# Streaming attention and an expert layer on one core: block order, load pieces and row sums changed

## The chip, the cores and the metric

The kernel runs on one core of a Trainium2 chip. The metric is the device time of one execution in microseconds, read as the median of the runs. The engines named below are TensorE (PE: matmuls and transposes), VectorE (DVE), ScalarE (ACT), GpSimd (POOL) and SyncE (SP, which here only issues transfers).

## What is computed

Four batches, eight heads, 768 positions, head size 64. Each query sees the 128 last positions and the first four ("sinks"). The result, 3072 tokens of 512, goes through four experts whose outputs are added with weights per token.

```python
keep = (pos[None, :] < 4) | ((rel >= 0) & (rel < 128))
scores = np.where(keep, scale * q @ k.T, -1e9)
a = exp(scores - max); a = a / (sum(a) + 1e-9)
x = (a @ v) as (tokens, 512)
p = domain_probs / (domain_probs.sum(-1) + 1e-9)
out = sum over e of p[:, e] * (relu(x @ w1[e]) @ w2[e])     # w1: 512x1024, w2: 1024x512
```

## The kernel before

**Tiling.** A *unit* `u` is one block of 128 queries of one batch with all eight heads; there are 24, six per batch. Before the change they run in the order of the output: unit 0 to 5 are batch 0, and so on. A block sees its own 128 keys and those of the block before it. Blocks 0 and 1 of a batch hold the sinks among these keys; block 0 has one key block instead of two. Blocks 2 to 5 need the four sink keys in addition.

**One unit.** `load` (L213) fetches q, k and v of the block, `[128, 8, 64]` float32, by three transfers of 256 KB on SyncE's queue, each row in pieces of 256 bytes. `cast` (L200) makes bf16 of them on GpSimd. For the first eight units (`UPE`, `UPA`, `UPX`) TensorE transposes queries and keys (`pe_tr`, L286; units 0 and 1 in float32 and without the cast), and `q_out`, `k_out` copy the result from PSUM; later units use transposing transfers (`dma_q`, `dma_k`). `scores` (L340) multiplies, `maxima` (L352, VectorE) masks and takes the minimum of the negated scores, `exps` (L360, ScalarE) forms the exponentials and, through `accum_out`, the row sums; this makes a second instruction, a reader, for each exp. `pe_a`/`a_out` (L400) or `dma_a` (L387) transpose the weights, `values` (L420) multiplies with V, `sums` and `normalise` divide, and `pe_x`/`x_out` (L471) or `dma_x` (L463) write the transposed result `xT`, 512 tokens (four units) to a tile.

**Sinks.** For units below `UPS` = 8 with block 2 or higher, the sinks' weights are transposed with the others and a 128x512 matmul (L417) with a spread matrix `vsd` adds their values; `vsd` is built from eight small loads (L240) and a GpSimd product (L160). From unit 8 on, `weigh_sinks` (L186, L190) does this on GpSimd from a broadcast copy `vsb` of the four values (1 MB per batch, L170), seven operations of 128x512.

**Experts.** Items are `(tokens, expert)`: first four items of 128 tokens with expert 0, then 512 tokens at a time. `mm1` (L495, tile `hpsum`), `relu` (L509, L507), `mm2` (L521, tile `mopsum`) and `collect` (L558 to L562) make one item. w1 and w2 of an expert are loaded by GpSimd's queue with a conversion to bf16 (L228, L231), each tied to a cast (`w_after`).

**What sets the order.** Every step is a node with a cost on an engine, its dependencies and a due time (`want`). A list scheduler written in the kernel takes the node that can start first by its own clock and emits the instructions in that order; `MOVED` holds hand-made shifts of due times, and loads, first and second matmuls keep fixed sequences. Where TensorE would idle at the start, `keep_busy` (L482) emits filler matmuls. Each engine runs its own list in order.

Of the kernel before, what the change touches and what calls it, by code (L numbers as in the profile page):

```python
# [16 lines left out]
def kernel(  # L17
# [43 lines left out]
    UPS = 8  # L61

    UG = 4

    UF = 2
# [12 lines left out]

    NBS = -(-(UPS - 2) // NQB)
    vs = resid.tile([HS, B, D], FP32, name="vs", tag="vs")  # L80
    vsd = [resid.tile([P, H, D], BF16, name=f"vsd{b}", tag=f"vsd{b}") for b in range(NBS)]
# [3 lines left out]
    dp_nat = consts.tile([NTB, P, E], FP32, name="dp_nat")  # L85


    Abuf = [resid.tile([P, 2 * H + 1, P], BF16, name=f"A{i}", tag=f"A{i}") for i in range(2)]
# [3 lines left out]
    qTb = [resid.tile([P, NHP, P], BF16, name=f"qT{i}", tag=f"qT{i}") for i in range(2)]  # L92
    skd = [resid.tile([P, NHP, 2, NSINK], BF16, name=f"skd{i}", tag=f"skd{i}") for i in range(2)]
# [48 lines left out]
    bd = consts.tile([HS, H], FP32, name="bd")  # L142

    def sink_consts(eng):
        for t in Abuf:
            nc.gpsimd.memset(t[:, 2 * H], 0.0)
        for t in vsd:
            nc.gpsimd.memset(t, 0.0)

# [3 lines left out]

    def sink_heads(eng):
        nc.vector.reduce_sum(
            out=bd, in_=ident[0:HS, 0:HS].rearrange("p (h r) -> p h r", r=NSINK), axis=AX.X
        )

    def sink_values(eng, b):
        nc.gpsimd.tensor_mul(  # L160
            vsd[b][0:HS], vs[:, b, :][:, None, :].to_broadcast([HS, H, D]),
            bd[:, :, None].to_broadcast([HS, H, D]),
        )
# [4 lines left out]
    def spread_values(eng, b):  # L168
        vsb[b] = at_sb.tile([P, H, NSINK, D], FP32, name="vsb", tag="vsb", bufs=1)
        nc.sync.dma_start(  # L170
            out=vsb[b].rearrange("p h r d -> p h (r d)"),
            in_=v[b, :, 0:NSINK, :].rearrange("h r d -> h (r d)")[None].to_broadcast(
                [P, H, NSINK * D]
            ),
        )

    def sinks_on_pool(u):
        return u >= UPS and u % NQB >= 2

    def weigh_sinks(eng, u):  # L180

        pr = Abuf[u % 2][:, 2 * H, 0:HS].rearrange("p (h r) -> p h r", r=NSINK)
        sv = at_sb.tile([P, H, D], FP32, name="sv", tag="sv", bufs=2)
        for r in range(NSINK):
            t = sv if r == 0 else at_sb.tile([P, H, D], FP32, name="svr", tag="svr", bufs=1)
            nc.gpsimd.tensor_mul(  # L186
                t, vsb[u // NQB][:, :, r], pr[:, :, r : r + 1].to_broadcast([P, H, D])
            )
            if r:
                nc.gpsimd.tensor_add(sv, sv, t)  # L190
        live["sv", u] = sv
# [26 lines left out]
    def cast(eng, u, what):  # L218
        t = raw.pop((what, u))
        if what == "v":  # L220
            vn[u] = resid.tile([P, H, D], BF16, name="vn", tag="vn", bufs=5)
            copy_on(eng, vn[u], t)
# [14 lines left out]

    def load_sinks(eng):
        for h in range(H):
            nc.sync.dma_start(  # L240
                out=vs[h * NSINK : (h + 1) * NSINK],
                in_=v[:, h, 0:NSINK, :].rearrange("b r d -> r b d"),
            )
# [23 lines left out]
    def queries_of(u):  # L267
        return qTb[u % 2]
# [6 lines left out]
    def dma_k(eng, u):  # L275
        b, qb = divmod(u, NQB)
# [5 lines left out]
    def pe_tr(eng, u, what):  # L282
        src = raw.pop((what, u)) if u < UF else nat.pop((what, u))
        ps = ps_s.tile([P, NHP, P], FP32 if u < UF else BF16, name="tr" + what, tag="s")
        for hp in range(NHP):
            nc.tensor.transpose(  # L286
                ps[:, hp], src[:, 2 * hp : 2 * hp + 2, :], identf if u < UF else ident
            )
        live["tr" + what, u] = ps

    def q_out(eng, u):
        copy_on(eng, qTb[u % 2], live.pop(("trq", u)))

    def k_out(eng, u):
        b, qb = divmod(u, NQB)
        copy_on(eng, keys_of(b)[:, :, qb], live.pop(("trk", u)))

    def sink_keys(eng, b):
        for c in range(2):
            r = slice(c * D, (c + 1) * D)  # L300
            copy_on(eng, skd[b % 2][r, :, c], kT[b][r, :, 0, 0:NSINK])

    def sink_scores(eng, u):
        ps = ps_s.tile([P, H, NSINK], FP32, name="ss", tag="s")
        for hp in range(NHP):
            nc.tensor.matmul(  # L306
                ps[:, 2 * hp : 2 * hp + 2], lhsT=qTb[u % 2][:, hp], rhs=skd[u // NQB % 2][:, hp],
# [23 lines left out]
    def scores(eng, u, g):  # L331

        b, qb = divmod(u, NQB)
        lo = 0 if qb else 1
        sp = {}
        for h in groups_of(u)[g]:
            if h % 2 not in sp:
# [3 lines left out]
                sp[h % 2][:, h // 2 % 2, lo:2], lhsT=qTb[u % 2][r, h // 2],  # L341
                rhs=kT[b][r, h // 2, qb - 1 + lo : qb + 1], start=True, stop=True,
# [3 lines left out]
    def maxima(eng, u, h):  # L346
        qb = u % NQB
        if ("negm", u) not in live:
            live["ssum", u] = at_sb.tile([P, H], FP32, name="ssum", tag="ssum", bufs=3)
# [8 lines left out]
    def exps(eng, u, h):  # L358
        lo = 1 if u % NQB == 0 else 0
        nc.scalar.activation(  # L360
            out=Abuf[u % 2][:, 2 * h + lo : 2 * h + 2, :], in_=SM[:, h, lo:2], func=AF.Exp,
            scale=-1.0, bias=live["negm", u][:, h : h + 1],
            accum_out=live["ssum", u][:, h : h + 1],
# [9 lines left out]
    def sink_exps(eng, u):  # L373
        nc.scalar.activation(  # L374
            out=Abuf[u % 2][:, 2 * H, 0:HS],
# [3 lines left out]
    def at_of(u):  # L379
        if ("AT", u) not in live:  # L380
            live["AT", u] = at_sb.tile([P, 2 * H + 1, P], BF16, name="AT", tag="AT", bufs=2)
        return live["AT", u]

    def dma_a(eng, u, half):
        lo = half * H
        hi = H if half == 0 else 2 * H + (1 if u % NQB >= 2 and not sinks_on_pool(u) else 0)
# [4 lines left out]
    def slots_of(u, hp):  # L391
        if hp == NHP:
            return [2 * H]
        return [4 * hp + i for i in range(4) if u % NQB > 0 or i % 2]
# [15 lines left out]
    def values(eng, u):  # L410
        b, qb = divmod(u, NQB)
        lo = 1 if qb == 0 else 0
        op = ps_s.tile([P, H, D], FP32, name="op", tag="s")
        at = live.pop(("AT", u))
        sinks = qb >= 2 and not sinks_on_pool(u)
        if sinks:
            nc.tensor.matmul(op, lhsT=at[:, 2 * H], rhs=vsd[b], start=True, stop=False)  # L417
        for h in range(H):
            for i in range(lo, 2):
                nc.tensor.matmul(  # L420
                    op[:, h], lhsT=at[:, 2 * h + i], rhs=vn[u - 1 + i][:, h, :],
                    start=(not sinks and i == lo),
                    stop=(i == 1 and (h == H - 1 or not sinks)),
                )
        live["op", u] = op

    def sums(eng, u):
        ssum = live.pop(("ssum", u))
        rs = at_sb.tile([P, H], FP32, name="rs", tag="rs", bufs=3)
        if u % NQB >= 2:  # L430
            rk = at_sb.tile([P, H], FP32, name="rk", tag="rk", bufs=3)
            nc.vector.reduce_sum(
                out=rk, in_=Abuf[u % 2][:, 2 * H, 0:HS].rearrange("p (h r) -> p h r", r=NSINK),
                axis=AX.X,
            )
            nc.vector.scalar_tensor_tensor(
                out=rs, in0=ssum, scalar=1e-9, in1=rk, op0=ALU.add, op1=ALU.add
            )
        else:
            nc.vector.tensor_scalar_add(rs, ssum, 1e-9)  # L440
# [3 lines left out]
    def normalise(eng, u):  # L444
        xn = at_sb.tile([P, H, D], BF16, name="xn", tag="xn", bufs=2)
        res = live.pop(("op", u))
        if sinks_on_pool(u):
            both = at_sb.tile([P, H, D], FP32, name="both", tag="both", bufs=1)
            nc.vector.tensor_add(both, res, live.pop(("sv", u)))  # L449
            res = both  # L450
        nc.vector.tensor_mul(  # L451
            xn, res, live.pop(("rs", u))[:, :, None].to_broadcast([P, H, D])
# [74 lines left out]
    def last_group(eng, i, sub):  # L527
# [4 lines left out]
        sc = live["shares"][:, tok // P, e : e + 1]  # L532
        at = 0
        for w, pool, tag in ((256, ps_o, "o"), (128, ps_h, "h"), (128, ps_o, "o")):
# [10 lines left out]
            nc.sync.dma_start(out=out[tok : tok + P, at : at + w], in_=dst[:, at : at + w])  # L545
            at += w

    def collect(eng, i, sub):
# [7 lines left out]
        sc = live["shares"][:, tok // P, e : e + 1]  # L556
# [9 lines left out]
    def store(eng, i, sub):  # L566
        tok = items[i][0] + sub * P
        nc.sync.dma_start(
            out=out[tok : tok + P, :], in_=out_sb[tok // 512][:, (tok % 512) // P, :]
# [32 lines left out]
    starts = [14.0, 20.0, 26.0, 32.0, 40.0, 56.0, 71.0]  # L602
# [12 lines left out]
    DMA_TILE = 0.19  # L615
    for u in range(NU):
        b, qb = divmod(u, NQB)
# [3 lines left out]
        for j, what in enumerate("qkv"):  # L621
            last = u - NRAW[what]
            free = ("cast", last, what)
            if last < UF and what != "v":
                free = ("tr" + what, last)
            deps = [(free, HOP)] if last >= 0 else []

            if u - AHEAD >= UPA:
                deps.append((("begun", "da", u - AHEAD, 1), HOP))
            node(("load", u, what), {"SP": 0.5}, lambda eng, u=u, w=what: load(eng, u, w), deps,  # L630
                 S0 - 24.0 + 0.1 * j, dma=1.0 if u < 2 else 1.1)
            deps = [(("load", u, what), HOP)]
            if u < UF and what != "v":
                continue
            if what == "v":
                if u >= 5:
                    deps.append((("av", u - 4), HOP))
            elif u >= UF + 2:
                prev = "tr" + what if u - 2 < UPE else "d" + what
                deps.append(((prev, u - 2), HOP))  # L640
            node(("cast", u, what), {"POOL": 0.56},
                 lambda eng, u=u, w=what: cast(eng, u, w), deps, S0 - 8.0 + 0.1 * j)
        qfree = [(("s", u - 2, len(groups_of(u - 2)) - 1), HOP)] if u >= 2 else []
        if u >= 2 and (u - 2) % NQB >= 2:
            qfree.append((("ss", u - 2), HOP))
        kfree = [(("s", (b - 1) * NQB - 1, 1), HOP)] if b >= 2 else []
# [390 lines left out]
```

## Time and profile before

| | |
|---|---|
| runs | 395.32, 502.31, 394.74 us; median 395.32 |
| profiled execution, span | 395.2 us, granted clock 1.000 |
| PE busy | 384.8 us (97%), 2513 instructions |
| DVE, ACT, POOL busy | 203.6 (52%), 225.6 (57%), 147.7 us (37%) |
| transfers | 51.95 MB in 148154 packets, 135548 of them under 512 bytes |

The page cuts the span into 40 slices and gives each engine's busy share in tenths. The chain of waits follows the work that ended last back to the start. A list in order of time has start, duration, engine, line, output and input, and in brackets the idle time ahead of an instruction and who ended it. A matmul's duration is longer than the distance to the next one, since they are pipelined.

### The profile page before, as it was taken

The numbers are of one execution on the slowest core, as the hardware profiler recorded it, in microseconds if no ns is written. First come the engines' busy times: TensorE is split into PE (matmuls) and PEld (weight loads), VectorE is DVE, ScalarE is ACT, GpSimd is POOL, SyncE is SP. The second block draws the span as 40 slices with busy tenths as digits, with TensorE's granted clock in tenths as the row PEclk, the third lists the DMA queues.
The fourth block names the chain that finished last, engine by engine and source line by source line (L and its number), as shares of the span: only waits on it lengthen the run. The fifth ranks groups of instructions, "written<-read, shape, count | busy, mean of one in ns | idle before, by whom it ended". The sixth has DMA issues, their size and how long they took to land.

```text
span 395.2 us, 7309 instructions
## 1 busy us (share of the span) xinstructions
PE 384.8 (97%) x2513; PEld 194.8 (49%) x2555; DVE 203.6 (52%) x672; ACT 225.6 (57%) x632; POOL 147.7 (37%) x177
## 2 busy tenths in 40 slices
PE   8999999999999999999999999999999999999996
PEld 6777555544444444444444444444444444444443
DVE  3996787259364853843866734456455332200233
ACT  5896787666573663764754746466377333354320
POOL 3515050309928561074495740154943800000000
PEclk9999999999999999999999999999999999999999
DMA  8998999918599689986555996762751300200002
GB/s 188 204 203 166 190 200 194 243 40 165 129 148 219 131 194 255 209 195 93 114 111 123 200 226 138 159 140 62 199 120 21 48 13 2 80 28 1 0 2 107
DMA packets 148154, 51.95 MB, mean 131 GB/s; under 512 B 135548, under 2 KB 143100, under 8 KB 148116
## 3 DMA queue, kind: packets, MB, share of 16 engines
q1 hardware_dynamic: 141844, 43.09, 51.2%
q0 software_dynamic: 6272, 8.39, 13.1%
q8 instruction: 20, 0.33, 0.3%
q14 instruction: 18, 0.15, 0.1%
HBM read 38.88 MB, written 6.29 MB: 114 GB/s over the span
## 4 chain that ended last, share of the span: by engine, by line
PE 86%; DMA 11%; issue 1%; POOL 1%; SPq 0%; DVE 0%; POOLq 0%
PE mopsum L521 40%; PE hpsum L495 39%; DMA rawk<-in_k_dram 5%; DMA rawv<-in_v_dram 5%; PE sp L340 3%; PE op L420 2%; DMA rawq<-in_q_dram 1%; PE lpsum L537 0%; PE tra L400 0%; PE trk L286 0%; PE trq L286 0%; PE ss L306 0%; POOL vn L200 0%; PE trx L471 0%; PE idle_out L482 0%
## 5 line engine op out<-in xcount | busy, mean ns | idle before, releaser
L495 PE MATMUL hpsum<-xT,w 128*128 128x512 bf16 (+1 forms) x843 | 182.5, 355 | 1.1
L521 PE MATMUL mopsum<-w,ht 128*128 128x512 bf16 x739 | 175.7, 379 | 1.6 <-issue 0.6
L509 ACT ACTIVATE ht<-hpsum 128x512 bf16<-128x512 f32 x172 | 102.0, 594 | 113.6 <-PE hpsum L495 100.8
L521 PEld LDWEIGHTS <-ht 128*128 128x128 bf16 x760 | 72.9, 98 | 87.7 <-issue 2.7
L495 PEld LDWEIGHTS <-w 128*128 128x128 bf16 x864 | 76.4, 98 | 79.0 <-issue 2.0
L562 DVE SCALAR_TENSOR_TENSOR out_sb<-mopsum,shares,out_sb 128x512 f32<-128x512 f32 x71 | 52.9, 746 | 109.2 <-PE mopsum L521 107.0
L360 ACT ACTIVATE A<-SM,negm 128x256 bf16<-128x256 f32 (+1 forms) x192 | 92.0, 481 | 16.6 <-DVE negm L352 13.6
L352 DVE CUSTOM_DVE_ANT_0 SM<-sp,M,slow 128x256 f32<-128x256 f32 x128 | 54.7, 479 | 8.6 <-PE sp L340 8.4
L190 POOL TENSOR_TENSOR sv<-sv,svr 128x512 f32<-128x512 f32 x36 | 45.6, 1267 | 2.8
L186 POOL TENSOR_TENSOR svr<-vsb,A 128x512 f32<-128x512 f32 x36 | 38.1, 1059 | 1.9
L200 POOL CAST qn<-rawq 128x512 bf16<-128x512 f32 x22 | 13.9, 634 | 62.1 <-DMA rawq<-in_q_dram 60.7
L360 ACT ACTIVATION_READ_ACCUMULATOR A<-SM,negm 128x1 f32 x192 | 36.3, 189 | 0.0
L186 POOL TENSOR_TENSOR sv<-vsb,A 128x512 f32<-128x512 f32 x12 | 13.0, 1082 | 62.5 <-ACT A L374 62.5
L558 ACT ACTIVATE out_sb<-mopsum,shares 128x512 f32<-128x512 f32 x19 | 13.0, 687 | 19.1 <-PE mopsum L521 19.0
L352 DVE CUSTOM_DVE_ANT_0 SM<-sp,M 128x128 f32<-128x128 f32 (+1 forms) x64 | 19.1, 351 | 5.9 <-PE sp L340 5.9
L200 POOL CAST kn<-rawk 128x512 bf16<-128x512 f32 x22 | 13.5, 614 | 19.7 <-DMA rawk<-in_k_dram 19.6
L200 POOL CAST vn<-rawv 128x512 bf16<-128x512 f32 x24 | 15.2, 633 | 12.5 <-DMA rawv<-in_v_dram 12.5
L449 DVE TENSOR_TENSOR both<-op,sv 128x512 f32<-128x512 f32 x12 | 8.3, 688 | 17.4 <-PE op L420 9.6
L340 PE MATMUL sp<-kT,qT 64*128 64x256 bf16 (+1 forms) x192 | 16.8, 271 | 0.0
L352 DVE DVE_READ_ACCUMULATOR2_ANT negm<- 128x1 f32 x192 | 15.9, 83 | 0.0
L420 PEld LDWEIGHTS <-AT 128*128 128x128 bf16 x352 | 13.4, 98 | 4.8 <-issue 0.2
L451 DVE TENSOR_TENSOR xn<-op,rs 128x512 bf16<-128x512 f32 x12 | 8.3, 688 | 14.5 <-PE op L420 14.1
(76 smaller groups left out, 197.5 us busy)
## 6 DMA issues: line engine op xcount, KB each, us to landing
w<-in_moe_w_dram POOLq DMA_DIRECT2D x8, 1024.0 KB, 12.8
rawq<-in_q_dram SPq DMA_DIRECT2D x24, 256.0 KB
rawk<-in_k_dram SPq DMA_DIRECT2D x24, 256.0 KB
rawv<-in_v_dram SPq DMA_DIRECT2D x24, 256.0 KB
out_dram<-out_sb SPq DMA_DIRECT2D x23, 256.0 KB
vsb<-in_v_dram SPq DMA_DIRECT2D x3, 1024.0 KB
AT<-A SPq DMA_TRANSPOSE x32
qT<-qn SPq DMA_TRANSPOSE x16
```

Of the source, the lines that this page charges most:

```text
L186: nc.gpsimd.tensor_mul(t, vsb[u // NQB][:, :, r], pr[:, :, r : r + 1].to_broadcast([P, H, D]))
L190: nc.gpsimd.tensor_add(sv, sv, t)
L200: nc.gpsimd.tensor_copy(out=out, in_=in_)
L340: nc.tensor.matmul(sp[h % 2][:, h // 2 % 2, lo:2], lhsT=qTb[u % 2][r, h // 2], rhs=kT[b][r, h // 2, qb - 1 + lo : qb + 1], start=True, sto ...
L352: nc.vector.tensor_tensor_reduce(out=SM[:, h][part], in0=live.pop(("sp", u, h))[part], in1=masks[min(qb, 2)], scale=-scale, scalar=live["s ...
L360: nc.scalar.activation(out=Abuf[u % 2][:, 2 * h + lo : 2 * h + 2, :], in_=SM[:, h, lo:2], func=AF.Exp, scale=-1.0, bias=live["negm", u][:, ...
L420: nc.tensor.matmul(op[:, h], lhsT=at[:, 2 * h + i], rhs=vn[u - 1 + i][:, h, :], start=(not sinks and i == lo), stop=(i == 1 and (h == H - ...
L495: nc.tensor.matmul(ps[:, j * n : (j + 1) * n], lhsT=w1[e][:, db, fb * P : (fb + 1) * P], rhs=xT[t0 // 512][:, db, t0 % 512 : t0 % 512 + n] ...
L509: nc.scalar.activation(out=ht, in_=ps, func=AF.Relu)
L521: nc.tensor.matmul(ps, lhsT=hidden(i, fb, sub), rhs=w2[e][:, fb, :], start=(fb == 0), stop=(fb == NFB - 1),)
L558: nc.scalar.activation(out=dst, in_=ps, func=AF.Copy, scale=sc)
L562: nc.vector.scalar_tensor_tensor(out=dst, in0=ps, scalar=sc, in1=dst, op0=ALU.mult, op1=ALU.add)
```

## The change

Six things change together.

- *Order.* Units 0 to 7 are now blocks 0 and 1 of batches 0 to 3; units 8 to 23 are blocks 2 to 5, batch by batch (`place`, `tile_of`). No unit below 8 needs sinks any more, and all 16 from unit 8 on take the GpSimd way: `vsd`, its loads and its matmul are gone, `vsb` is loaded four times instead of three. Keys and values of the first blocks are kept until their batch's turn (`kside`, `vk`, `move_keys`).
- *Loads.* q and k of two blocks come in one transfer of 512 KB, in pieces of 512 bytes; a partition then holds two neighbouring rows, and `every_other` puts the transposed columns back in order.
- *First units.* Units 0 and 1 are cast to bf16 like the others, on any of three engines, ahead of the transposes.
- *Row sums below unit 8.* V gets a 65th column of ones; `values` runs by halves of four heads, and `normalise_half` reads the sum from the product. The exps of these units have no `accum_out`.
- *Weights.* w1 and w2 are tied to other casts (`w_at`); q of unit 4 waits for w2 of expert 0, q of unit 6 for w1 of expert 1 (`BEHIND`).
- *Due times.* `starts`, `MOVED` and some costs of nodes have new numbers.

```diff
+    BEHIND = {4: ("w2", 0), 6: ("w1", 1)}
...
+    def place(u):
+        if u < UPS:
+            return divmod(u, 2)
+        b, qb = divmod(u - UPS, NQB - 2)
+        return b, qb + 2
...
     def sinks_on_pool(u):
-        return u >= UPS and u % NQB >= 2
+        return u >= UPS
...
     def load(eng, u, what):
-        b, qb = divmod(u, NQB)
-        t = resid.tile([P, H, D], FP32, name="raw" + what, tag="raw" + what, bufs=NRAW[what])
+        b, qb = place(u)
+        if u < UPS and what != "v":
+            t = resid.tile([P, 2 * H * D], FP32, name="raw" + what, tag="raw" + what, bufs=NRAW[what])
+            for j in range(2):
+                raw[what, u + j] = t.rearrange("p (h j d) -> p h j d", h=H, j=2)[:, :, j]
+            nc.sync.dma_start(
+                out=t.rearrange("p (h x) -> p h x", h=H),
+                in_=src_of[what][b, :, 0 : 2 * P, :].rearrange("h (p j) d -> p h (j d)", j=2),
+            )
+            return
...
+            full = resid.tile([P, H, D + 1], BF16, name=tag, tag=tag, bufs=bufs)
+            if u < UPS:
+                nc.gpsimd.memset(full[:, :, D : D + 1], 1.0)
+            copy_on(eng, full[:, :, 0:D], t)
...
+    def every_other(t, u):
+        return t.rearrange("p a s (c j) -> p j a (s c)", j=2)[:, u % 2]
...
     def q_out(eng, u):
-        copy_on(eng, qTb[u % 2], live.pop(("trq", u)))
+        copy_on(eng, every_other(qTb[u // 2 % 2], u), live.pop(("trq", u)))
...
+        total = {"accum_out": live["ssum", u][:, h : h + 1]} if u >= UPS else {}
...
+    def values(eng, u, heads=range(8)):
+        blocks = [(1, u)] if before(u) is None else [(0, before(u)), (1, u)]
+        w = D + 1 if u < UPS else D
+        op = ps_s.tile([P, len(heads), w], FP32, name="op", tag="s")
...
+    def normalise_half(eng, u, f):
+        op = live.pop(("op", u, 4 * f))
+        rs = at_sb.tile([P, 4], FP32, name="rsh", tag="rsh", bufs=3)
+        nc.vector.tensor_scalar_add(rs, op[:, :, D], 1e-9)
+        nc.vector.reciprocal(out=rs, in_=rs)
+        nc.vector.tensor_mul(
+            live["xn", u][:, 4 * f : 4 * f + 4], op[:, :, 0:D],
+            rs[:, :, None].to_broadcast([P, 4, D]),
+        )
...
-    w_after = [(2, "v"), (3, "v"), (4, "v"), (5, "v"), (6, "v"), (7, "v"), (10, "v"), (11, "v")]
+    w_at = [(2, 'q'), (3, 'q'), (3, 'v'), (4, 'v'), (6, 'q'), (6, 'k'), (8, 'k'), (12, 'q')]
```

More of the change, by code (lines that the diff above doesn't have):

```diff
@@ L385, in dma_a @@
         lo = half * H
-        hi = H if half == 0 else 2 * H + (1 if u % NQB >= 2 and not sinks_on_pool(u) else 0)
+        hi = lo + H
         nc.sync.dma_start_transpose(
@@ L615, with avs, norms, last_s @@
     DMA_TILE = 0.19
+    LOAD1 = 1.15
+    LOAD2 = 1.85
+    def avs(u):
+        return [("av", u, 0), ("av", u, 1)] if u < UPS else [("av", u)]
+    def norms(u):
+        return [("norm", u, 0), ("norm", u, 1)] if u < UPS else [("norm", u)]
+    def last_s(u):
+        return ("s", u, len(groups_of(u)) - 1)
+    def all_exps(u):
+        return [("exp", u, h) for h in range(H)]
+    def on(*lists):
+        return [(key, HOP) for keys in lists for key in keys]
+    rawat = {"q": [], "k": [], "v": []}
+    vnat = []
     for u in range(NU):
-        b, qb = divmod(u, NQB)
+        b, qb = place(u)
         pe = u < UPE
@@ L621 @@
         for j, what in enumerate("qkv"):
[L622 to L631, printed above, removed]
@@ L639 @@
+            deps = [(("load", u // 2 * 2 if pair else u, what), HOP)]
+            if what == "v":
+                if u >= UPS or u % 2 == 0:
+                    if len(vnat) >= NVN:
+                        deps += on(avs(vnat[-NVN]))
+                    vnat.append(u + 1 if u % 2 == 0 and u < UPS else u if qb == NQB - 1 else u + 1)
+            elif u >= 2:
                 prev = "tr" + what if u - 2 < UPE else "d" + what
                 deps.append(((prev, u - 2), HOP))
-            node(("cast", u, what), {"POOL": 0.56},
+            node(("cast", u, what),
+                 {"POOL": 0.56, "DVE": 0.38, "ACT": 0.58} if u < 2 and what != "v" else {"POOL": 0.66 if u < UPS and what == "v" else 0.56},
@@ L647 @@
+        kfree = on([last_s(UPS + 4 * (b - 2) + 3)]) if b >= 2 and u >= UPS else []
         if pe:
             for what in "qk":
[L649 to L654 removed]
@@ L658 @@
+            node(("ko", u), any_of(0.5, 0.36), lambda eng, u=u: k_out(eng, u),
+                 on([("trk", u)]), S0 - 2.0)
+            have = on([(x, 2 * (u // 2) + j) for x in ("qo", "ko") for j in range(2)])
         else:
@@ L821 @@
     node(("shares",), {"DVE": 0.8}, shares_out, [(("trs",), HOP)], 9.0)
-    MOVED = {
[4 rows of a table removed]
-    }
+    MOVED = {'ao': 6.8,
+     'da': -3.8,
+     'dq': 2.8,
+     'dx': -2.0,
+     'exp': 3.8,
+     'i0': -4.1,
+     'i1': 1.8,
+     'i10': -6.1,
+     'i11': -6.7,
+     'i2': 15.0,
+     'i3': 6.1,
+     'i4': 5.5,
+     'i5': 8.8,
+     'i6': -1.9,
+     'i7': 5.0,
+     'i9': -6.8,
+     'mm1': 0.5,
+     'mm2': 1.7,
+     'norm': -5.3,
+     'out': -7.2,
+     'relu': 15.1,
+     's': -8.2,
+     'ska': -30.8,
+     'sm': -3.5,
+     'ss': 1.0,
+     'sv': -0.9,
+     'trk': -7.2,
+     'trq': -2.9,
+     'u0': -9.9,
+     'u1': 1.6,
+     'u11': -2.2,
+     'u12': -18.9,
+     'u13': 9.5,
+     'u15': 10.9,
+     'u4': -31.5,
+     'u5': 12.8,
+     'u6': 16.9,
+     'u7': 4.5,
+     'u9': -3.6,
+     'x': 3.1,
+     'xT': -6.7}
     for key, d in nodes.items():
@@ L832 @@
             d["want"] += MOVED.get(f"i{key[1]}", 0.0) + MOVED.get(key[0], 0.0)
-        elif len(key) > 1 and key[0] not in ("w1", "w2", "load", "sk", "vsd", "vsb"):
+        elif len(key) > 1 and key[0] not in ("w1", "w2", "load", "sk", "kc", "vsb"):
             if key[1] < 9:
```

324 lines of the change are left out of this document (148 added, 176 removed), and 4 rows, old and new, of the table MOVED.

## The prediction

> **What bounds the kernel now.** I read the busy table by slices first, then TensorE's list in order of time, then the DMA and queue rows of the first 40 us. The profiled execution took 395.2 us, the median of the runs shown is 395.32; the sum is made against 395.2.
>
> ```profile
> PE   8999999999999999999999999999999999999996
> PEclk9999999999999999999999999999999999999999
> DMA  8998999918599689986555996762751300200002
> PE mopsum L521 40%; PE hpsum L495 39%; DMA rawk<-in_k_dram 5%; DMA rawv<-in_v_dram 5%; PE sp L340 3%; PE op L420 2%; DMA rawq<-in_q_dram 1%; PE lpsum L537 0%; PE tra L400 0%; PE trk L286 0%; PE trq L286 0%; PE ss L306 0%; POOL vn L200 0%; PE trx L471 0%; PE idle_out L482 0%
> ```
>
> The reader is to see that TensorE is full at the full granted clock (first and second row), and that all transfers on the chain of waits belong to q, k and v. They lie at its start. So the questions are how early useful matmuls start, how many there are, and where TensorE waits. Three places in TensorE's list, and the table by stretches:
>
> ```profile
> 26.46 0.72 PE L495 MATMUL hpsum<-xT,w 128*128 128x128 bf16 x10
> 67.59 0.59 PE L495 MATMUL hpsum<-xT,w 128*128 128x512 bf16 x2
> 389.59 1.93 PE L537 MATMUL lpsum<-w,ht 128*128 128x256 bf16 x24
> ...
> 20.00:30.00 10.00, 9.27 (x141) 7.45 (x138) 9.36 (x41) 10.00 (x36) 1.03 (x1) 1.00 1.18 204
> 67.59:391.50 323.91, 321.74 (x1838) 151.07 (x1872) 152.39 (x456) 172.47 (x454) 126.02 (x133) 1.00 0.57 119
> ```
>
> The first expert matmul stands at 26.46, the third weight set (w1 of expert 2) is first used at 67.59, the last matmul ends at 391.5, and 3.7 us follow for the last store. From 20 to 30 us VectorE (9.36) and ScalarE (10.00) are full as well and DMA is over its 16 engines; from 67.59 on every engine but TensorE is about half idle.
>
> I price each matmul by the distance from start to start in the list: 128x512 0.216 us (8 in 1.73), 128x128 0.056, scores of 256 columns 0.068 (8 in 0.54), op 0.029, float32 transposes 0.24, the fillers of L482 0.107. Summed over the instruction order this gives 372.5 us of useful work, 11.7 of it ahead of the first hpsum, and 79 fillers, all ahead of it (8.45 us). So TensorE's unfilled waits are: 26.46 - 1.1 - 11.7 - 8.45 = 5.2 us ahead of the first hpsum; 41.13 - 39.0 = 2.1 us from there to 67.59; 323.9 - 321.8 = 2.1 us in all the rest. Only the first part has much to give.
>
> **The change, part by part.**
>
> *TensorE's work.* The 16 float32 transposes become bf16: 16 x (0.24 - 0.056) = -2.9 us. The four 128x512 sink matmuls of L417 go: -0.9. Four units instead of two are first blocks, which need 8 instead of 16 transposes of the weights (116 to 96): -1.1. Scores, op and experts keep their counts. New sum 367.6 us. In the new order 7.4 us of it and 80 fillers (8.56) stand ahead of the first hpsum, 360.15 behind it (before: 360.75).
>
> *The first hpsum*, three chains. (a) TensorE's own row: 1.1 + 7.4 + 8.6 + the same 5.2 of waits = 22.3. (b) VectorE. Its first masked minimum starts at 7.04 now. A pair of 512 KB takes longer than one block: a stretch that holds only 256-byte pieces shows its rate.
>
> ```profile
> GB/s 174 169 220 215 261 256 287 251 261 297 282 292 282 292 297 282 297 272 297 297 272 297 276 297 287 276 282 276 297 292 282 266 271 246 236 195 200 225 184 205
> DMA packets 2071, 0.52 MB, mean 261 GB/s; under 512 B 2071, under 2 KB 2071, under 8 KB 2071
> ```
>
> 261 GB/s from 10 to 12 us, so 1.0 us for 256 KB. Pieces of 512 B are bounded by this (2.0 us a pair) and by 70 to 72 us, where two thirds of the packets are larger (334 GB/s, 1.57 us); I take 1.75, in the middle. So k lands 1.5 us later than now, a cast (0.61, L200 row) and a second copy (0.4) come in, float32 transposes save 0.9: first minimum at 8.6. Then, by steps of the DVE rows: unit 0 and unit 2 minima 2 x 8 x 0.21, unit 1's 8 x 0.35, half of unit 3's 1.4, five copies 1.4, one xT copy 0.34, four half normalisations of 0.75: 12.3 us, and 2.6 of gaps as now (19.4 us hold 16.8 of work): 23.5. ScalarE is shorter: without the 0.19 us readers of L360 an exp steps 0.30 or 0.41 instead of 0.39 or 0.49. (c) The weights of expert 0.
>
> ```profile
> 12.96 0.61 POOL L200 CAST vn<-rawv 128x512 bf16<-128x512 f32 x1 [0.29 <-DMA rawv<-in_v_dram]
> 13.52 0.94 POOL L228 DMA_DIRECT2D w<-in_moe_w_dram  x1
> 18.22 0.89 POOL L231 DMA_DIRECT2D w<-in_moe_w_dram  x1
> 30.83 0.61 POOL L200 CAST qn<-rawq 128x512 bf16<-128x512 f32 x1 [6.39 <-DMA rawq<-in_q_dram]
> ```
>
> w1 is issued at 13.52, behind nine loads, and lands 11.8 us later (25.3); w2 is issued at 18.22 and lands at 32.0. In the new POOL order w1 stands behind the casts of unit 2 and 3's queries, w2 right behind it. Ahead of those casts lie three pairs and two v: 3 x 1.75 + 2.0 = 7.25 us instead of 9.0 (the offset is 12.96 - 9.0 = 3.9), with two casts: issued at 12.3. The landing took 10.1 to 15.6 us in the seven rows up to 110 us; with three loads left beside it instead of five I take 10.5: 22.8. The three chains give 22.3 to 23.5; I take 22.7, so -3.8 us, and 20.0 to 25.0 as ends.
>
> VectorE's copies into qT and kT now write every second element, which no row shows. They lie between 0.42 us (the bf16 copy of qT) and 0.69 (the same from float32), and two k copies are on chain (b); I take 0.42, as the type is the same. At the other end (b) is 24.0. The Trainium skill, "VectorE: DVE Perf Modes", section "Mode 2×_1P — pack two bf16 into one 32-bit read", asks for step 1 for two results a cycle; by it the copies would run at the 0.69 of the float32 row.
>
> *Work behind the first hpsum:* 360.15 - 360.75 = -0.6.
>
> *Waits from there to w1 of expert 2.* New is that unit 4's pair waits for the whole w2 of expert 0, and unit 6's for w1 of expert 1 (BEHIND). On SyncE's queue unit 4's v and unit 6 stand behind them; those casts in turn hold the issue of the next weights on POOL. w2 lands 6.7 us behind w1 now, so at 29.4; its first use is 7.1 us of work behind the first hpsum, at 30.2: covered by 0.8. w1 of expert 1 follows to 36.1 and is used at 38.0. Unit 4's keys land between 33.9 (nothing beside them) and 39.6 (all behind w1), cast at most 1.2 later; TensorE wants them transposed at 39.0. So 0 to 1.8 of new wait: +0.7.
>
> *The rest.* GpSimd weighs sinks for 16 units instead of 12, 8.3 us each (88.75 to 97.05), +33 us; with casts a unit takes 10 of the 15 us per unit that TensorE gives it. VectorE gains four adds of 0.69. The one-buffer vsb is now reloaded between neighbouring units, a 1 MB transfer with GpSimd idle; SyncE's queue holds next loads and xT behind it. In the new order the last op of the last unit stands 9 us of work ahead of its first hpsum (before: 11), so a late sum is mostly hidden; uncovered, 3 us a batch. Taken: +0.5. The eight small loads of vs (5 us of SyncE's queue) and vsd on GpSimd go; they lie beside other work: 0. So do the small additions: eight fewer load issues on SyncE (0.4 to 1.5 us each), on GpSimd eight memsets of the ones column and two key copies of 0.6, under its 11 busy us of 41 in the early stage.
>
> *Sum:* 395.2 - 3.8 - 0.6 + 0.7 + 0.5 = 392.0 us.
>
> **The rivals.** *A, the start is much earlier.* Pieces of 512 B come at the larger-packet rate, w1 lands at 20, and two of the 5.2 us waits go with the readers: first hpsum at 20.0, and the waits to w1 of expert 2 halve: 395.2 - 6.5 - 0.6 - 1.1 = 387.0. For it: ScalarE and VectorE are full ahead of 26.46 and both get less. Against: chain (b), where the pair makes k later. The Trainium skill, "DMA: Bandwidth & Descriptors", section "Specifications", puts the least size for line rate at 512 B; by that rule this rival comes out.
>
> *B, the loads behind the weights starve.* Unit 4's q was issued at 17.98 and could be cast only at 30.83, 12.9 us, with two weight transfers in flight. The change makes this regular. Unit 4 from 29.4: keys at 42.3, w2 of expert 1 issued at 43.5, landing 14.4 later (as its row now) at 57.9, wanted at T+26.4 of work or 51.5: 6.5 us, and one more at w1 of expert 2: 392.0 - 0.7 + 7.5 = 398.8, slower than before. It decides from a landing of unit 4's keys past 41. For: that row. Against: one weight transfer is in flight then, not two.
>
> *C, the change does little:* pieces of 512 B are no faster and the copies slow; chain (b) gives 24.7 for the first hpsum: 394.0. *D, GpSimd becomes the bound* in the last batches through vsb: three reloads at 3 us uncovered: 401. Against: 65% load.
>
> **How the numbers follow.** Forecast 0.48 (its own range 389 to 394), A 0.18, B 0.18, C 0.11, D 0.05. The range, 386.5 to 400, takes in A and B and leaves out the tails beyond, about 0.18. A change of 2%, 7.9 us, is about what a measurement of this kernel can tell from no change: below 387.4 lies A and a little of the forecast's tail, 0.20; above 403.2 only the far ends of B and D, 0.12; the rest, 0.68, lies within.
>
> **What would show it.** Right: first hpsum at 21.5 to 24, w1 of expert 2 first used near 61, then 325 us of work with 2 to 3 us of waits; DMA rows of the pairs at about 300 GB/s; exps without readers below unit 8. Wrong: first hpsum before 20.5 (A), a wait of TensorE on kn or w between 30 and 65 over 3 us (B), VectorE waiting on sv repeatedly ahead of an hpsum late in the trace (D).

## The result, and the profile after

The changed kernel takes 402.33 us (402.23 to 402.55), the kernel before 395.22: a ratio of 1.018, with a 95% interval of [1.017, 1.020]. It is 7 us slower; the forecast was 3 us less than before. Now and then a run lies more than 1.5% above the fastest of its kernel (502.31 us before the change, 411.31 in one set below); the ratios leave such runs out. The profiled execution took 402.35 us at a span of 400.6. First the rows by slices, with the share of the chain of waits:

```profile
PE   6999999999999989999999999998999999999996
PEclk9689999999999999999999999999999999999999
DMA  9999999903949999996498696359668022100003
...
PE hpsum L515 32%; PE mopsum L541 32%; POOL sv L187 4%; POOL svr L183 3%; DMA w<-in_moe_w_dram 3%; PE sp L355 2%; DMA xT<-xn 2%; DMA rawq<-in_q_dram 2%; PE op L436 2%; ACT A L377 1%; PE tra L414 1%; DMA rawk<-in_k_dram 1%; DMA rawv<-in_v_dram 1%; POOL sv L183 1%; DVE SM L368 1%
```

TensorE is still full in nearly every slice, but the clock row has a 6 and an 8 in the first three, and the chain now holds GpSimd's sums of the sinks (sv, svr: 8%), w and xT, of which the chain of before had none. TensorE's list and the table by stretches, for the places shown of before:

```profile
25.45 1.89 PE L515 MATMUL hpsum<-xT,w 128*128 128x128 bf16 x16
62.46 0.81 PE L515 MATMUL hpsum<-xT,w 128*128 128x512 bf16 x3
394.90 1.93 PE L558 MATMUL lpsum<-w,ht 128*128 128x256 bf16 x24
...
20.00:30.00 10.00, 9.43 (x105) 7.21 (x105) 8.26 (x46) 8.30 (x24) 1.25 (x3) 0.83 1.18 211
62.46:396.80 334.34, 329.51 (x1949) 154.62 (x1947) 176.53 (x523) 175.40 (x463) 159.76 (x162) 1.00 0.61 117
```

The first expert matmul starts 1.0 us earlier than before (25.45 for 26.46; forecast 22.7), w1 of expert 2 is first used 5.1 us earlier (62.46 for 67.59; forecast 61), and the rest takes 10.4 us longer: 334.34 us with 4.8 of idle, where before had 323.91 with 2.2. Some 3.4 of the 10.4 are work that the earlier use moves behind this point (at the prediction's prices 325.1 us stand behind it for 321.8); the other 7 us are lost there. So the loss lies behind 62 us. TensorE's list of the changed kernel there, its waits of over 0.2 us (idle time and who ended it in brackets):

```profile
75.71 0.28 PE L491 MATMUL trx<-ident,xn 128*128 128x128 bf16 x2 [0.46 <-DVE xn L449]
117.22 0.38 PE L355 MATMUL sp<-kT,qT 64*128 64x256 bf16 x3 [0.74 <-DVE sneg L328]
143.09 0.60 PE L541 MATMUL mopsum<-w,ht 128*128 128x512 bf16 x2 [1.24 <-DMA w<-in_moe_w_dram]
212.19 0.60 PE L515 MATMUL hpsum<-xT,w 128*128 128x512 bf16 x2 [0.22 <-DMA xT<-xn]
277.08 1.24 PE L515 MATMUL hpsum<-xT,w 128*128 128x512 bf16 x5 [1.11 <-DMA xT<-xn]
316.09 0.38 PE L355 MATMUL sp<-kT,qT 64*128 64x256 bf16 x3 [0.81 <-DVE sneg L328]
```

Three different releasers: VectorE's minima of the next unit, w2 of expert 3, and the transposed xT. What stands behind VectorE's lateness is in its own list:

```profile
114.78 0.69 DVE L470 TENSOR_TENSOR sv<-op,sv 128x512 f32<-128x512 f32 x1 [3.71 <-POOL sv L187]
115.51 0.89 DVE L471 TENSOR_TENSOR xn<-sv,rs 128x512 bf16<-128x512 f32 x1
116.32 0.74 DVE L583 SCALAR_TENSOR_TENSOR out_sb<-mopsum,shares,out_sb 128x512 f32<-128x512 f32 x1
116.99 0.18 DVE L328 TENSOR_SCALAR sneg<-ss 128x32 f32<-128x32 f32 x1
```

VectorE takes its work in order. The addition of unit 9's sink values (L470) waits 3.71 us for GpSimd's sum, and sneg of the next unit, which needs nothing of it, stands three places behind; TensorE's scores wait for it until 117.22. In all VectorE waits 30.1 us for sv in this trace, 7.8 before (total, times and longest wait; the changed kernel first):

```profile
DVE sv L470 <- POOL sv L187: 30.1, 10, 6.1
...
DVE both L449 <- POOL sv L190: 7.8, 4, 6.1
```

### The profile page after: what moved, and what is told of

Read it like the earlier page. It is cut to its first block, busy times and chain, and to the rows that moved or that the text cites. A ratio compares the mean times of both kernels' runs of the same rounds, so it can differ in the third digit from the quotient of the medians.

```text
span 400.6 us, 7236 instructions
## 1 busy us (share of the span) xinstructions
PE 387.4 (97%) x2532; PEld 193.6 (48%) x2532; DVE 217.1 (54%) x703; ACT 217.6 (54%) x560; POOL 181.6 (45%) x217
## 4 chain that ended last, share of the span: by engine, by line
PE 71%; DMA 9%; POOL 9%; DVE 4%; ACT 2%; issue 2%; SPq 1%; POOLq 0%; ACTq 0%
PE hpsum L515 32%; PE mopsum L541 32%; POOL sv L187 4%; POOL svr L183 3%; DMA w<-in_moe_w_dram 3%; PE sp L355 2%; DMA xT<-xn 2%; DMA rawq<-in_q_dram 2%; PE op L436 2%; ACT A L377 1%; PE tra L414 1%; DMA rawk<-in_k_dram 1%; DMA rawv<-in_v_dram 1%; POOL sv L183 1%; DVE SM L368 1%
## 5 line engine op out<-in xcount | busy, mean ns | idle before, releaser
L515 PE MATMUL hpsum<-xT,w 128*128 128x512 bf16 (+1 forms) x864 | 184.8, 357 | 1.6 <-DMA xT<-xn 1.3
L541 PE MATMUL mopsum<-w,ht 128*128 128x512 bf16 x760 | 177.5, 379 | 1.2 <-DMA w<-in_moe_w_dram 1.2
L529 ACT ACTIVATE ht<-hpsum 128x512 bf16<-128x512 f32 x168 | 99.8, 595 | 110.8 <-PE hpsum L515 108.7
L377 ACT ACTIVATE A<-SM,negm 128x256 bf16<-128x256 f32 (+1 forms) x192 | 88.2, 484 | 26.6 <-DVE negm L368 26.3
L187 POOL TENSOR_TENSOR sv<-sv,svr 128x512 f32<-128x512 f32 x48 | 60.9, 1269 | 3.8
L183 POOL TENSOR_TENSOR sv<-vsb,As 128x512 f32<-128x512 f32 x16 | 17.6, 1103 | 78.3 <-ACT As L390 64.4
L183 POOL TENSOR_TENSOR svr<-vsb,As 128x512 f32<-128x512 f32 x48 | 50.8, 1058 | 2.5
L470 DVE TENSOR_TENSOR sv<-op,sv 128x512 f32<-128x512 f32 x16 | 11.1, 691 | 32.0 <-POOL sv L187 30.1
L377 ACT ACTIVATION_READ_ACCUMULATOR A<-SM,negm 128x1 f32 x128 | 24.4, 191 | 0.0
L527 DVE TENSOR_SCALAR ht<-hpsum 128x512 bf16<-128x512 f32 x24 | 16.5, 688 | 2.7 <-PE hpsum L515 2.5
```

The source lines that it names most:

```text
L183: nc.gpsimd.tensor_mul(t, vsb[place(u)[0]][:, :, r], pr[:, :, r : r + 1].to_broadcast([P, H, D]))
L377: nc.scalar.activation(out=Abuf[u % 2][:, 2 * h + lo : 2 * h + 2, :], in_=SM[:, h, lo:2], func=AF.Exp, scale=-1.0, bias=live["negm", u][:, ...
L515: nc.tensor.matmul(ps[:, j * n : (j + 1) * n], lhsT=w1[e][:, db, fb * P : (fb + 1) * P], rhs=xT[t0 // 512][:, db, t0 % 512 : t0 % 512 + n] ...
L527: nc.vector.tensor_scalar_max(out=ht, in0=ps, scalar1=0.0)
L529: nc.scalar.activation(out=ht, in_=ps, func=AF.Relu)
L541: nc.tensor.matmul(ps, lhsT=hidden(i, fb, sub), rhs=w2[e][:, fb, :], start=(fb == 0), stop=(fb == NFB - 1),)
```

## The experiments

The kernels ran in four sets, each beside the kernel before on the same chip (396.39, 395.89, 396.35 and 396.12 us); every ratio below is to that of its own set. Medians resolve about 1 us, so a single wait is read in the trace.

**Both kernels again.** No edit.

> The kernel before, unaltered, for a second profile. The profile that the prediction was summed against had a span of 395.2 us; the runs of this kernel on another chip had spans of 393.4 to 398.0 and times 1.7 above their spans. Expected: span 393.4 to 394.5, the difference to 395.2 ahead of the first hpsum (26.46) if the start varies, or behind 67.59 if waits appear by chance.

> The changed kernel itself, unaltered, as the measure for the three others on the same chip. Expected 401 to 403, with TensorE's waits of over 0.3 us behind unit 7 at 76, 117, 143, 277 and 316 us again; if they are a matter of chance, others appear instead.

395.59 us (span 393.9) and 403.23 us, 1.020 [1.017, 1.022]. In every run the time lies 1.65 to 1.86 us above the span. So the profile that the prediction summed against, at a span of 395.2, was one of about 396.9 us; the second profile lacks a wait of 0.91 us for kn at 52.6 and starts its experts 0.3 earlier. TensorE's lists of before (first three lines) and of the changed kernel (last three), both from these runs:

```profile
26.13 1.06 PE L495 MATMUL hpsum<-xT,w 128*128 128x128 bf16 x16
31.99 1.89 PE L521 MATMUL mopsum<-w,ht 128*128 128x512 bf16 x8
388.27 1.93 PE L537 MATMUL lpsum<-w,ht 128*128 128x256 bf16 x24
```

```profile
24.86 1.89 PE L515 MATMUL hpsum<-xT,w 128*128 128x128 bf16 x16
33.11 1.67 PE L541 MATMUL mopsum<-w,ht 128*128 128x512 bf16 x7
394.73 1.93 PE L558 MATMUL lpsum<-w,ht 128*128 128x256 bf16 x24
```

The last group of matmuls starts 6.46 us later. Up to the first hpsum the changed kernel gains 1.27; from there to the first mopsum it loses 2.39 (8.25 us for 5.86: 1.2 more work in between, and 1.2 beyond price at half clock, where the first 16 matmuls take 1.89 us instead of 1.06); behind it 5.34 (361.62 for 356.28), although its order holds 1.8 us less work there (353.1 for 354.9 by the prediction's prices). Behind the first mopsum, gaps of over 0.35 us beyond price come to 6.0 us in the changed kernel; the kernel before has none. The waits at 75, 117, 142, 277 and 316 us are there again; that at 212 is not, and one of 0.27 us at 153 is new.

**GpSimd's work alone.**

```diff
-        for r in range(NSINK):
+        for r in range(1):
```

> Leaves out sinks 1 to 3 of the four in GpSimd's sums (one multiplication a unit instead of four and three additions, 1.05 us instead of 8.3 to 8.7); the order of everything else stays. Theory G (the late waits of TensorE, 0.5 + 0.3 + 0.9 + 1.3 + 0.3 + 1.2 + 0.95 = 5.4 us at 76, 103, 117, 143, 212, 277 and 316 us, come from GpSimd's sums: VectorE's next unit and the issue of w2 of expert 3 are queued behind them): all of them go, 402.3 - 5.4 = 397, between 396 and 398. Theory R (the reload of vsb sets them, not the sums): waits at 212 and 277 stay, 401 or more. Theory S (the written order and the start alone cost the time): 402 within 0.6.

399.70 us, 1.008 [1.006, 1.011]. The waits at 103, 117, 212 and 316 are gone, and VectorE's wait for GpSimd with them (that at 103 was 0.13 us of idle in the changed kernel); the one for w2 of expert 3 (1.64), that at 277 (1.51) and that at 76 (0.46) stay. Theory G is right for the scores and wrong for two transfers and for the wait at 76. w2 was issued at 129.0 instead of 132.1 and landed only 0.4 us earlier (142.6 for 143.0). SyncE's queue (start, time of the issue) with TensorE's wait last:

```profile
263.31 0.53 SPq L167 DMA_DIRECT2D vsb<-in_v_dram  x1
263.89 0.63 SPq L223 DMA_DIRECT2D rawq<-in_q_dram  x1
264.57 2.33 SPq L223 DMA_DIRECT2D rawk<-in_k_dram  x1
266.95 4.44 SPq L223 DMA_DIRECT2D rawv<-in_v_dram  x1
271.49 1.51 SPq L483 DMA_TRANSPOSE xT<-xn  x1
...
276.62 0.59 PE L515 MATMUL hpsum<-xT,w 128*128 128x512 bf16 x2 [1.51 <-DMA xT<-xn]
```

The wait at 277 is not one of GpSimd at all. Behind the 1 MB of vsb the issues of k and v take 2.33 and 4.44 us, and the transposing transfer of xT, four places behind vsb, is issued only at 271.49.

**The reload of vsb.** In `spread_values`:

```diff
+        if b:
+            vsb[b] = vsb[0]
+            return
```

> Loads vsb once and leaves out the three reloads (all batches use the sink values of the first). Theory G: GpSimd's sums stay 8.3 to 8.7 us a unit, only the waits at 212 and 277 us go, 402.3 - 1.5 = 400.8. Theory R: most of the late waits go, 398.5 or less. Theory S: 402 within 0.6.

401.44 us, 1.010 [1.006, 1.015]: the waits at 212 and 277 are gone, 117, 143 and 316 stay. xT is issued at 267.27 instead of 272.01 (SyncE's queue of this run):

```profile
264.33 0.57 SPq L226 DMA_DIRECT2D rawq<-in_q_dram  x1
264.95 0.62 SPq L226 DMA_DIRECT2D rawk<-in_k_dram  x1
265.61 1.04 SPq L226 DMA_DIRECT2D rawv<-in_v_dram  x1
267.27 1.20 SPq L486 DMA_TRANSPOSE xT<-xn  x1
```

The waits are as theory G had them, the reason is the queue.

**The same with the right values.** In `spread_values`:

```diff
-        vsb[b] = at_sb.tile([P, H, NSINK, D], FP32, name="vsb", tag="vsb", bufs=NVS)
-        nc.sync.dma_start(
+        for c in {0: (0, 1), 1: (2,), 2: (3,), 3: ()}[b]:
+            vsb[c] = at_sb.tile([P, H, NSINK, D], BF16, name="vsb", tag="vsb", bufs=2)
+            nc.gpsimd.dma_start(
```

> vsb is held in bf16, in two buffers in the same space, and loaded through GpSimd's queue one batch ahead; SyncE's queue no longer carries it; all other instructions keep their order. Theory Q (a vsb of 1 MB ahead on SyncE's queue holds back the loads and the transposing transfers of xT behind it, and GpSimd waits for it): the waits at 212 and 277 us go, those at 76, 117, 143 and 316 stay: 1.3 to 1.7 us below the unaltered kernel. Theory G (all late waits come from GpSimd's sums): nothing or under 0.5 us. If a bf16 operand makes GpSimd's multiplications shorter than 1.05 us, 117 and 316 go as well: up to 3.5 us.

402.21 us, 1.015 [1.013, 1.018]; 1.0 us less than the unaltered kernel of the same set, within its uncertainty. In the trace 212 and 277 are gone, 117 and 316 stay, as theory Q has it; the wait for w2 of expert 3 is 1.85 us here instead of 1.22. A bf16 operand leaves GpSimd's multiplication at 1.05 us.

**w2 of expert 3.** In `load_w1`, with the node of w2 of expert 3 issuing nothing:

```diff
+        if e == E - 1:
+            load_w2(eng, e, early=True)
```

> The transfer of w2 of expert 3 is issued right behind that of w1 of expert 3 on GpSimd's queue instead of behind the cast of unit 12's queries (132.1 us); all other instructions keep their order. Theory W: the wait of the first mopsum of expert 3 (1.24 to 1.40 us at 143 us) goes and nothing takes its place: 402.3 - 1.3 = 401.0. Rival: the two transfers hold back the loads of units 9 and 10, or the next wait for the sinks grows by as much: 402 to 403.

401.80 us, 1.011 [1.006, 1.017]. The wait at 143 is gone; those at 117, 211, 276 and 315 stay as they were.

**The clock.** The table by stretches of the changed kernel (the third figure from the right is the granted clock, ahead of DMA share and GB/s):

```profile
7.00:10.80 3.80, 2.11 (x29) 1.43 (x29) 2.59 (x12) 1.26 (x4) 2.31 (x7) 1.00 1.27 253
10.80:17.70 6.90, 6.76 (x56) 4.71 (x56) 6.13 (x34) 6.78 (x19) 6.14 (x12) 0.51 1.24 248
24.50:27.90 3.40, 3.40 (x33) 2.79 (x33) 2.76 (x11) 2.53 (x7) 0.00 (x0) 0.50 1.20 210
```

From 24.5 to 27.9 TensorE is fully busy and at half clock; `keep_busy` got twice the fillers:

```diff
-                keep_busy(int(gap * FILL / 0.107), halves)
+                keep_busy(int(gap * FILL / (0.0535 if st > 4.0 else 0.107)), halves)
```

> Twice the fillers for the gaps that the order expects from 4 us on (52 more matmuls of L502, none of them behind the first mopsum). Theory C (TensorE dropped to half clock at 10.8 to 17.7 and at 24.5 to 27.9 us because it was too little busy in the stretches before): full clock from 4 us on, hpsum at 25 us in 0.95 us instead of 1.68, time 402.3 - 1.3 = 401.0. Rival: the half clock comes whatever the fillers do, 402.3. Second rival: the fillers run at half clock (0.107 us) and delay the transposes of units 1 to 3: up to 5 us later, 404 to 407.

400.62 us, 1.010 [1.007, 1.013]. In the profiled run the clock is full from 5.7 us on, and the first 16 hpsum are shorter, though they start later:

```profile
25.86 1.07 PE L515 MATMUL hpsum<-xT,w 128*128 128x128 bf16 x16
```

Runs lie between 398.95 and 403.06, those of over 402 at a mean clock of 0.991, the best at 0.999. Six of the ten have a mean clock of 0.999 or 1.000; none of the eight runs of the unaltered kernel is above 0.994. So more fillers make the half clock rarer and don't secure the clock in each run. Two parts of theory C aren't shown. That TensorE was too little busy before the stretch at 24.5 is not: from 17.7 to 24.5 it was busy for 6.13 of 6.80 us, and with the fillers doubled for 6.33. Nor is 400.62 the price of the clock alone: the waits at 212 and 277 are absent from this trace too, though vsb is loaded as before (xT is issued at 270.66), so these two depend on about a microsecond of timing. The Trainium skill, "TensorE: Matmul & The Clock Gate", section "Part 1: The HAM clock gate (the "warmup" mystery)", says that the state follows TensorE's activity in windows of about 3.4 us and differs from run to run; the stretches here are of 3.4 and 6.8 us and begin at 10.8, 11.8 or 23.9 in different runs, which agrees.

**The strided copies.**

```diff
-        copy_on(eng, every_other(qTb[u // 2 % 2], u), live.pop(("trq", u)))
+        copy_on(eng, qTb[u // 2 % 2][:, :, u % 2], live.pop(("trq", u)))
```

(the same for k.)

> The copies of q and k of units 0 to 7 out of PSUM write whole runs of 128 columns instead of every second column; left out is the order of the tokens within a pair of blocks. Order, transfers and all other work stay. Theory P (the strided copies, 0.73 us on VectorE and 0.74 on ScalarE instead of 0.42 and 0.58, are what mis-sized the start): the first masked minimum 0.3 to 0.6 earlier than 9.8, the first hpsum 1 to 2 us earlier than 25.5, the time 1 to 2 us below the unaltered kernel. Rival (the start is set by the pairs' casts, w1's landing or the half clock, and the copies lie beside): within 0.6 us of it.

401.84 us, 1.015 [1.013, 1.017], 1.4 us less than the unaltered kernel. VectorE's groups of the changed kernel (mean ns behind the bar), then VectorE's and TensorE's lists of this run:

```profile
L195 DVE COPY qT<-trq 128x512 bf16<-128x512 bf16 x2 | 1.3, 722 | 0.5 <-PE trq L296 0.5
L195 DVE COPY AT<-tra 128x512 bf16<-128x512 bf16 x3 | 1.3, 425 | 0.2 <-PE tra L414 0.2
```

```profile
8.05 0.76 DVE L195 COPY kT<-trk 128x512 bf16<-128x512 bf16 x2 [1.02 <-PE trk L296]
8.83 0.29 DVE L368 CUSTOM_DVE_ANT_0 SM<-sp,M 128x128 f32<-128x128 f32 x1
...
24.06 0.71 PE L515 MATMUL hpsum<-xT,w 128*128 128x128 bf16 x5 [0.48 <-DMA w<-in_moe_w_dram]
```

A strided copy takes 0.72 us, a plain one 0.42. Without the strides the first masked minimum starts at 8.83 (9.76 in the unaltered run, 8.6 forecast) and the first hpsum at 24.06, where it now waits for w1: the next limit is 0.8 us away. Theory P holds, with other sizes: the first minimum is 0.93 us earlier (0.3 to 0.6 expected), the first hpsum 0.8 (1 to 2 expected).

**The pairs undone.** With the plain copies, and in `load`:

```diff
-                in_=src_of[what][b, :, 0 : 2 * P, :].rearrange("h (p j) d -> p h (j d)", j=2),
...
+            for w, j in [("q", 0)] if what == "q" else [("k", 0), ("q", 1), ("k", 1)]:
...
+                    in_=src_of[w][b, :, j * P : (j + 1) * P, :].rearrange("h p d -> p h d"),
```

> q and k of units 0 to 7 are loaded block by block again (256-byte pieces, q, k of the first block, then of the second) and copied in whole runs; place, the ones column and the sums stay, the result is the reference's. Theory U (the pair costs the start: k of unit 0 lands behind 1 MB instead of 0.5 MB): first masked minimum near 8, 1.5 to 2 us earlier than 9.8, first hpsum 1.5 to 3 us earlier than 25.5, time 2 us below the unaltered kernel. Rival (the pairs' rate, 335 to 346 GB/s at 3 to 4.5 us against the 261 of 256-byte pieces, is worth more than the delay): w1 of expert 0 is issued 1 us or more later than 12.5 and the time is the same or up to 2 us above.

407.59 us, 1.027 [1.022, 1.032]. By the runs that the ratio takes (median 406.75) it is 4.9 us more than the version with plain copies and pairs. w1 is issued at 14.76 instead of 12.50, and the first hpsum starts at 27.11. Theory U is wrong: the first minimum starts later (10.6); that casts and transposes keep the order written for pairs may be why, and was not tried. In the changed kernel the transfers move, from 3 to 6 us:

```profile
GB/s 355 328 314 369 348 362 335 335 348 369 355 341 328 341 362 342 328 348 314 287 307 294 280 300 300 273 300 294 273 300 300 273 300 287 287 294 307 328 297 273
```

Some 345 GB/s while pairs are alone, against the 261 of 256-byte pieces. The rule of the Trainium skill, "DMA: Bandwidth & Descriptors", section "Specifications", that puts the least size for line rate at 512 bytes, agrees.

**A new order for the measured sums.**

```diff
-            node(("sv", u), {"POOL": 7.3}, ...
+            node(("sv", u), {"POOL": 8.7}, ...
```

> The order is made anew with 8.7 us instead of 7.3 for GpSimd's sums of the sinks (measured 8.3 to 8.7); nothing else changes, but many instructions change places. Theory O (the waits at 117 and 316 come from an order that takes the sums for shorter than they are, so that VectorE's addition is queued ahead of the next unit's minima too early): both go, 1.5 to 2 us below 403.2. Rival (the other due times were set for the old order, and other waits appear): 402 to 405.

412.00 us, 1.040 [1.037, 1.043]. The waits at 117 and 316 go, as theory O says, and a larger one comes. SyncE's queue, TensorE's wait, and the table by stretches:

```profile
264.48 11.20 SPq L403 DMA_TRANSPOSE AT<-A  x4
275.77 1.02 SPq L167 DMA_DIRECT2D vsb<-in_v_dram  x1
...
284.54 1.51 SPq L483 DMA_TRANSPOSE xT<-xn  x1
```

```profile
288.62 0.61 PE L515 MATMUL hpsum<-xT,w 128*128 128x512 bf16 x1 [6.04 <-DMA xT<-xn]
...
285.70:292.50 6.80, 3.88 (x10) 1.41 (x11) 0.00 (x0) 0.85 (x2) 6.41 (x7) 0.50 1.22 234
```

xT stands behind vsb and three loads again, TensorE waits 6.04 us, and the clock falls to half 3.1 us into the wait, for 6.8 us, so that the work behind it is slowed as well. So this cost of the order can't be corrected alone; that the due times (`MOVED`), made for the old cost, are why is likely and was not tried.

**All causes taken away.** Fillers doubled from 13 us on (17 more), w2 of expert 3 with w1, vsb in bf16 through GpSimd's queue, and the last addition of the sinks on VectorE, its summand in bf16 (parts of the edit):

```diff
-            if r:
+            if r and r < NSINK - 1:
                 nc.gpsimd.tensor_add(sv, sv, t)
...
         nc.vector.tensor_add(both, live.pop(("op", u, 0)), both)
+        nc.vector.tensor_add(both, both, live.pop(("svr", u)))
```

> The changed kernel with every cause taken away that the runs have shown: twice the fillers from 13 us on (17 more), w2 of expert 3 issued behind its w1, vsb in bf16 in two buffers through GpSimd's queue, and the last of the three additions of the sinks on VectorE (GpSimd 1.27 us less a unit, VectorE 0.7 more). If these are all: the waits at 76 (0.45) and small rests are left, 403.2 - 1.0 (half clock at 24 to 27) - 1.3 (w2) - 1.5 (vsb) - 1.2 to 1.8 (117 and 316) = 397.9, between 396.5 and 399, the kernel before being at 395.9. If late waits only move (VectorE or GpSimd becomes late at other units): 399.5 to 402.

397.98 us, 1.004 [1.001, 1.006], as expected (397.9). All named waits but that at 75 are gone, for two new ones:

```profile
88.81 0.26 PE L324 MATMUL ss<-skd,qT 128*128 128x8 bf16 x4 [1.33 <-DMA qT<-qn]
104.68 0.59 PE L521 MATMUL hpsum<-xT,w 128*128 128x512 bf16 x2 [0.77 <-DVE ht L533]
```

**The last step.** The same, with w2 of expert 3 and the second vsb behind unit 8's sums (102 and 103 us).

> As the version with all causes taken away, but w2 of expert 3 and the second vsb are issued on GpSimd's queue behind the first sums of the sinks (unit 8, near 103 us) instead of at 72 and 57 us, where other transfers were in flight. Theory T (the new wait of 1.33 us for unit 9's transposed queries at 89 us came from loads held back behind these two transfers): it goes, 398.0 - 1.3 = 396.7, within 1 of the kernel before. Rival (it belongs to the order, and w2 issued at 103 lands too late or the wait for it moves): 398 or more.

404.94 us, 1.024 [1.020, 1.028]. The wait at 89 goes, so theory T is right on its origin; but the two transfers now lie beside unit 9's transposed A, for which TensorE waits:

```profile
114.53 0.61 PE L442 MATMUL op<-vn,AT 128*128 128x64 bf16 x8 [4.28 <-DMA AT<-A]
...
113.10:119.90 6.80, 5.37 (x20) 2.22 (x21) 2.08 (x3) 1.19 (x2) 1.23 (x2) 0.50 1.32 202
```

A wait of 4.28 us, and again the clock halves within it (2.9 us after it began), for 6.8 us. That the two transfers hold back that of A is read from where they lie and was not varied. No version was found that beats the kernel before.

## Why the prediction was wrong

*What bounds the kernel* was read rightly: TensorE, its start and its waits. But the sum stood on a span, and the span is 1.7 us below the time; and that profile was of a run 1.6 us over the median, with a wait of 0.9 us in it that the second profile lacks. By luck the two slips cancel: the difference of -3.2, set against the median's own span of 393.6 and raised to a time, gives 392 as well.

*TensorE's work* (372.5 to 367.6) is right in count and worth little: 3.1 of the 4.9 us lay ahead of the first mopsum, where TensorE waits for VectorE and weights in any case. In the second pair of profiles it gets there with 3.1 us less work behind it, and 1.1 us later than before.

*The first hpsum*, -3.8 us, was mis-sized: -1.0 in the profiled run, -1.3 in the second pair. All three chains must end, so the sum had to take the longest of its own three (23.5), not 22.7 from between them. The copies ran beyond the 0.69 end and not at the 0.42 taken; without strides the first hpsum is 0.8 us earlier. The rule of the Trainium skill, "VectorE: DVE Perf Modes", section "Mode 2×_1P — pack two bf16 into one 32-bit read", which asks for step 1 for two results a cycle, was the right one: 0.72 us with the strides, 0.42 without; ScalarE's copies, for which no other end was given, rose from 0.58 to 0.74 too. w1 landed at 24.0 in the run without strides, not at 22.8. The price of a pair, 1.75 us, was high: at 345 GB/s it is 1.5. And no term allowed for the clock: at half clock from 24.5 to 27.9 the first 16 matmuls took 0.8 us more, and in the second profile the way to the first mopsum took 1.2 more.

*Waits to w1 of expert 2*: better than forecast. From the first hpsum to it 37.0 us passed for some 35 of work (38.3 from the forecast's 22.7 to its 61). No single wait of TensorE reaches 0.15 us there, so rival B did not come, and no wait shows that BEHIND cost anything. Two times on paper don't add up: 22.7 and 7.1 make 29.8 for the first use of w2 and not 30.2, and rival B's 51.5 doesn't follow from 22.7 and 26.4.

*"The rest", +0.5 us*, is the step that failed: it took late waits for hidden. Behind the first use of w1 of expert 2 the changed kernel loses 8.8 us beyond 325.4 us of work (the forecast had 325), the kernel before in its second profile 2.2: 6.6 us more, where 0.5 was taken. The step named GpSimd's 33 us more, vsb between neighbouring units and xT behind it on SyncE's queue, and called them hidden because a unit takes 10 of the 15 us that TensorE gives GpSimd and the last op stands 9 us ahead. These were means. Single waits decided, by their idle time in the first trace: scores behind VectorE's addition (0.74 and 0.81 us) and xT behind vsb (0.22 and 1.11). Two more it did not name at all: w2 of expert 3, tied to the cast of unit 12's queries (1.24), and unit 7's halves of the normalisation (0.46). Together they are 4.6 us of idle, and the five of them that came back in the second profile 4.7. The edits show the origin of the waits at 117, 143, 277 and 316 us; that at 212 comes and goes by itself, and that at 75, unit 7's, no run varied.

*Rival D* had 0.05 and came nearest: 401, with vsb as its cause. The number was luck in part, its mechanism half right: vsb did cost, but through the queue of SyncE behind it (0.22 and 1.11 us of waits) and not through GpSimd's idle time, and more came from VectorE's queue behind sv, from w2 and from the clock. *Rival A*'s rate was right (345 GB/s; undone, 4.9 us are lost), but the start hung on copies and casts. *Rival C*'s first hpsum of 24.7 is about what came, but C had no late waits. The signs named for a wrong forecast showed: VectorE waits on sv repeatedly, and 4.8 us of idle stand where 2 to 3 were to be.

The version without these causes is where the sum of their prices put it (397.98 for 397.9). What stays open: it is still 1.6 us above the kernel before (396.35). Two new waits of 2.1 us are seen in it; whether an order written for it would lose them was not tried.

## What to carry to other kernels

Where several chains must end, the latest one is the sum; and work taken off an engine ahead of the point where it waits for others was worth nothing here. A mean load of 65% says little of a queue taken in order: for each wait that a change adds, list the next three instructions on that engine and who needs them, and for each large transfer what is issued behind it on its queue. A due time or a transfer moved by itself in an order that was tuned as a whole can cost more than the wait that it removes.

## What the runs showed of the hardware

In waits of TensorE of 4.3 and 6.0 us in the middle of full work the clock fell to half 2.9 and 3.1 us after the wait began and stayed there for 6.8 us (113.1 to 119.9 and 285.7 to 292.5); in waits of up to 1.85 us it did not. The Trainium skill, "TensorE: Matmul & The Clock Gate", section "HAM oscillation — how this bites in real kernels", tells of the same for waits that cross a window, which agrees. Issues of k and v on SyncE's queue took 2.3 to 4.4 us each behind a transfer of 1 MB, 0.6 to 1.0 at the same place without it. ScalarE too pays for a write of every second element out of PSUM: 0.74 us instead of 0.58 for 128x512 in bf16.
